# A fused attention and two-MLP kernel: statistics of the first MLP off VectorE's one-column operations, moe_w_out's scaling in one instruction, ScalarE's tables preloaded

## The chip, the core and the metric

The kernel runs on one core of a Trainium2 chip. The time is the device time of one execution in microseconds (us), the median of several runs. A profile is one execution recorded by the hardware profiler; its span runs from the first to the last instruction. TensorE is PE in the rows (PEld its weight loads), VectorE is DVE, ScalarE is ACT, GpSimd is POOL, and SP is the engine that issues the DMAs. L12 is line 12 of the kernel.

## The reference

Attention with a compressed memory (4 batches, 8 heads, 576 tokens, width 64) gives 2304 rows of 512 columns. Two MLPs follow. Only the first is touched:

```
h = x @ w_in                                   # 2304 x 1024
e = exp(h - max(h)); sm = e / (sum(e) + 1e-9)
solu = h * sm
mu = mean(solu); var = mean((solu - mu)**2)
ln = (solu - mu) / sqrt(var + 1e-6) * g_ln
x = ln @ w_out                                 # 2304 x 512
```

The second is `(sigmoid(x @ w_gate) * (x @ w_val)) @ w_out`. The weights arrive as 64-bit floats.

## The kernel before

Every matmul takes its operands as a high and a low part in fp32r and sums three products. The work has three stages: attention in 16 head pairs in a fixed order (up to 219 us), the first MLP (to 440 us), the second MLP in 6 passes over its width (to the end).

The first MLP (class `Moe1`) works in 18 tiles of 128 tokens. `hidden(t)` splits the input (`xs`, L594 on ScalarE, L595 on GpSimd for t below 6 and on VectorE after), multiplies it by w_in into a PSUM tile `h` (L602, 24 matmuls, two PSUM buffers), and takes the statistics: maximum (L609, VectorE), exp with its sum (L611, ScalarE), then sum plus 1e-9 and its reciprocal (L612, L613, VectorE, one column each), product with h and its sum (L615, VectorE; this read is the last one of the PSUM tile), minus the mean (L616, one column), squares and their sum (L619, ScalarE), variance plus 1e-6 (L620, VectorE, one column), the power -0.5 (L622, GpSimd, one column), mean times that (L623, VectorE, one column), and the normalised tile (L624, ScalarE). `lntrans(t)` transposes it on TensorE (L641, `pl`) and splits it into `lnT` (L138 on ScalarE, L139 on VectorE); `proj(g)` multiplies two tiles by w_out (L653, `po`).

Beside the first tiles runs the conversion of w_out (`w_out`, 8 blocks of 128x512, two staging buffers `raw` and `ex`): a DMA, two integer masks (L108, L109, VectorE), the exponent (L112, ScalarE), two products on VectorE (L119 mantissa, L117 exponent), then per block g_ln's scaling and the product of mantissa and exponent: for odd blocks both on GpSimd (L574, L575), for even ones the scaling on ScalarE (L577) and the product on GpSimd (L578). Then the high part (L580, ScalarE) and the low part `wol` (L145, GpSimd). The weights of the second MLP are converted in the same way later (L703 on VectorE, L142 and L145 on GpSimd).

The attention stage is written in its final order. After it a scheduler sets each engine's order from its own estimates; every engine then works through its queue in that order. `gl` holds g_ln: it is loaded by a DMA (L799) and scaled on VectorE (L800), and both come to stand in the attention stage.

Of the kernel before, what the change touches and what calls it, by code (L numbers as in the profile page):

```python
# [8 lines left out]
F32 = mybir.dt.float32  # L9
# [4 lines left out]
AF = mybir.ActivationFunctionType  # L14
ALU = mybir.AluOpType
AX = mybir.AxisListType
# [19 lines left out]
def f32(ap):  # L36
    return ap.bitcast(F32)
# [13 lines left out]
def kernel(  # L51
# [16 lines left out]
    nc = tc.nc  # L68
    B, H, S, D = q.shape
    NT, DM = out.shape  # L70
    F1 = moe_w_in.shape[1]
    F2 = moe2_w_gate.shape[1]
    P = 128
# [12 lines left out]
    cpool = ctx.enter_context(tc.tile_pool(name="cpool", bufs=1))  # L86
# [2 lines left out]
    make_identity(nc, ident)  # L89
    mhalf = cpool.tile([P, 1], F32, tag="mhalf", name="mhalf")  # L90
    nc.vector.memset(mhalf, -0.5)

    ebias = cpool.tile([P, 1], F32, tag="ebias", name="ebias")
    nc.vector.memset(ebias, -896.0 * 2.0**23)
# [29 lines left out]
    def load_f64(raw, ex, mt, src):  # L124
        load_raw(raw, src)
        f64_a(raw, ex, mt)
        f64_r(ex)
        f64_b(raw, ex, mt)
# [15 lines left out]
    def pool_lo(lo, src, hi):  # L144
        nc.gpsimd.tensor_sub(lo, src, f32(hi))  # L145
# [400 lines left out]
    class Moe1:  # L546
# [15 lines left out]
        def w_out(self, wp, stage, gl):  # L562

            self.wo = []
            for c in range(NF1):
                self.wo.append(
                    [wp.tile([P, DM], F32R, tag=f"wo{x}{c}", name=f"wo{x}{c}") for x in "hl"]
                )

            def one(c):  # L570
                raw, ex, m = staged(stage, f"wo{c}")
                load_f64(raw, ex[:, 0], ex[:, 1], moe_w_out[c * P : c * P + P, :].unsqueeze(1))
                if c % 2:
                    nc.gpsimd.tensor_scalar(m, m, gl[:, c : c + 1], 1.0, ALU.mult, ALU.mult)  # L574
                    nc.gpsimd.tensor_mul(m, m, f32(ex[:, 0]))  # L575
                else:
                    nc.scalar.activation(m, m, AF.Copy, scale=gl[:, c : c + 1])  # L577
                    nc.gpsimd.tensor_mul(m, m, f32(ex[:, 0]))  # L578
                hi, lo = self.wo[c]
                nc.scalar.copy(hi, m)  # L580
                pool_lo(lo, m, hi)

            return [lambda c=c: one(c) for c in range(NF1)]

        def hidden(self, t):
            sb = self.sb
            xs = self.xe.tile([P, 2, NC, P], F32R, tag="xs", name=f"xs{t}")
            e = self.xe.tile([P, F1], F32, tag="e", name=f"e{t}")
            ph = self.ps.tile([P, F1], F32, tag="h", name=f"h{t}", bufs=2)

            def xsplit():
                hi, lo = (xs[:, i].rearrange("p c (n t) -> p n c t", t=64) for i in range(2))
                src = X[:, 2 * t : 2 * t + 2]
                nc.scalar.copy(hi, src)  # L594
                (nc.gpsimd if t < 6 else nc.vector).tensor_sub(lo, src, f32(hi))  # L595

            def mm(c):
                hi, lo = self.wi[c]
                for s, ws in ((0, (hi, lo)), (1, (hi,))):
                    for w in ws:  # L600
                        for j in range(2):
                            nc.tensor.matmul(  # L602
                                ph[:, j * 512 : j * 512 + 512], xs[:, s, c], w[:, j * 512 : j * 512 + 512],
                                start=(c == 0 and s == 0 and w is hi), stop=(c == NC - 1 and s == 1),
                            )

            def stats():
                nm = sb.tile([P, 1], F32, tag="hm", name=f"hm{t}", bufs=2)
                self.last = nc.vector.tensor_reduce(nm, ph, axis=AX.X, op=ALU.max, negate=True).ins  # L609
                sm = sb.tile([P, 1], F32, tag="sm", name=f"sm{t}", bufs=2)  # L610
                nc.scalar.activation(e, ph, AF.Exp, bias=nm, accum_out=sm)  # L611
                nc.vector.tensor_scalar_add(sm, sm, 1e-9)  # L612
                nc.vector.reciprocal(sm, sm)  # L613
                mu = sb.tile([P, 1], F32, tag="mu", name=f"mu{t}", bufs=2)
                nc.vector.scalar_tensor_tensor(e, ph, sm, e, ALU.mult, ALU.mult, accum_out=mu)  # L615
                nc.vector.tensor_scalar_mul(mu, mu, -1.0 / F1)  # L616
                va = sb.tile([P, 1], F32, tag="va", name=f"va{t}", bufs=2)
                sq = sb.tile([P, F1], BF16, tag="sq", name=f"sq{t}", bufs=1)
                nc.scalar.activation(sq, e, AF.Square, bias=mu, accum_out=va)  # L619
                nc.vector.tensor_scalar(va, va, 1.0 / F1, 1e-6, ALU.mult, ALU.add)  # L620
                rd = sb.tile([P, 1], F32, tag="rd", name=f"rd{t}", bufs=2)
                nc.gpsimd.tensor_tensor(rd, va, mhalf, ALU.pow)  # L622
                nc.vector.tensor_mul(mu, mu, rd)  # L623
                nc.scalar.activation(e, e, AF.Identity, bias=mu, scale=rd)  # L624
                self.ln[t] = e

            return [xsplit, *(lambda c=c: mm(c) for c in range(NC)), stats]
# [157 lines left out]
    def staged(pool, nm):  # L785
        raw = pool.tile([P, 512, 2], I32, tag="raw", name=f"raw{nm}")
        ex = pool.tile([P, 2, 512], I32, tag="ex", name=f"ex{nm}")
        return raw, ex, f32(ex[:, 1])
# [4 lines left out]
    gl = cpool.tile([P, NF1], F32, tag="gl", name="gl")  # L793
# [63 lines left out]
```

## Time and profile before

| | us |
|---|---|
| median of 3 runs | 900.95 |
| lowest and highest | 899.72, 902.34 |
| the profiled execution, its time | 900.28 |
| its span | 898.4 |
| TensorE busy | 869.9 (97%) |
| VectorE busy | 555.1 (62%) |
| ScalarE busy | 419.4 (47%) |
| GpSimd busy | 273.1 (30%) |

Busy shares are means over three stages with different limits. A matmul's end is modelled, so a busy TensorE is not one at its peak. What a stage is worth is read from that stage's own waits.

### The profile page before, as it was taken

The page shows a single profiled execution, that of the slowest core. Times are in us where ns is not written, and L with a number is a line of the kernel's source. Part 1 is how long each engine was busy: PE and PEld are TensorE (multiplying, and loading weights), DVE is VectorE, ACT ScalarE, POOL GpSimd, SP SyncE. Part 2 cuts the span into 40 slices and gives each one's busy share as a digit, 9 for nine tenths or more (in the row PEclk, how much of TensorE's full clock was granted, in tenths as well). Part 3 has the DMA queues.
Part 4 walks back from the last instruction along what each step waited for, and adds up shares of the span by engine and source line. Part 5 has one row for each costly group of instructions (what it writes and reads, how often), then busy time and mean ns, then how long its engine had stood idle before and what let it go on. Part 6 is the DMA issues. An engine that isn't in the chain of part 4 may idle for free.

```text
span 898.4 us, 13966 instructions
## 1 busy us (share of the span) xinstructions
PE 869.9 (97%) x5224; PEld 724.4 (81%) x5224; DVE 555.1 (62%) x1317; ACT 419.4 (47%) x925; POOL 273.1 (30%) x320
## 2 busy tenths in 40 slices
PE   5999999999789999999999999999999999999998
PEld 3777777766678999999898888888888888888887
DVE  5899999995775554948642168365359635343334
ACT  4899999995765555654453242112113111111110
POOL 3777777784744111204200042040025012000000
PEclk9999999999979999999999999999999999999999
DMA  5543444420212000301200022011003100000113
GB/s 118 114 107 91 112 98 107 116 85 25 71 48 71 24 25 24 92 4 49 93 2 0 1 94 94 1 48 47 1 24 117 48 0 1 1 1 1 47 47 117
DMA packets 76291, 48.62 MB, mean 54 GB/s; under 512 B 62656, under 2 KB 62656, under 8 KB 76224
## 3 DMA queue, kind: packets, MB, share of 16 engines
q1 hardware_dynamic: 76224, 47.74, 19.1%
q8 instruction: 41, 0.67, 0.3%
q14 instruction: 26, 0.21, 0.1%
HBM read 43.00 MB, written 4.72 MB: 53 GB/s over the span
## 4 chain that ended last, share of the span: by engine, by line
PE 88%; DVE 6%; POOL 2%; issue 1%; DMA 1%; ACT 1%; SPq 0%; POOLq 0%; DVEq 0%; ACTq 0%
PE gv L735 33%; PE po L754 16%; PE po L653 9%; PE h L602 7%; PE x L464 5%; PE sc L355 4%; PE x L449 2%; PE sc L346 1%; PE pl L641 1%; PE trk L265 1%; PE trq L265 1%; PE trf L265 1%; DVE hm L609 1%; DVE exwo L119 1%; DVE exwo L108 1%
## 5 line engine op out<-in xcount | busy, mean ns | idle before, releaser
L741 DVE TENSOR_TENSOR sg<-sg,gv 128x512 f32<-128x512 f32 (+1 forms) x60 | 37.9, 632 | 176.6 <-ACT sg L740 176.6
L740 ACT ACTIVATE sg<-gv 128x512 f32<-128x512 f32 (+1 forms) x60 | 33.1, 552 | 234.5 <-PE gv L735 234.5
L735 PE MATMUL gv<-xx,gh 128*128 128x512 f32 (+1 forms) x480 | 136.1, 368 | 0.2 <-ACT xx L138 0.2
L735 PE MATMUL gv<-xx,vh 128*128 128x512 f32 (+1 forms) x480 | 136.0, 368 | 0.0
L653 PE MATMUL po<-lnT,woh 128*128 128x256 f32 x576 | 107.2, 288 | 3.8 <-DVE lnT L139 3.0
L735 PEld LDWEIGHTS gv<-xx,gh 128*128 128x128 f32 x480 | 87.4, 188 | 16.1 <-issue 0.4
L735 PEld LDWEIGHTS gv<-xx,vh 128*128 128x128 f32 x480 | 87.1, 189 | 15.0
L653 PEld LDWEIGHTS po<-lnT,woh 128*128 128x128 f32 x576 | 92.2, 195 | 5.6 <-DVE lnT L139 3.4
L394 POOL TENSOR_SCALAR p<-p,rs,o 128x256 f32<-128x256 f32 (+2 forms) x144 | 91.8, 652 | 11.6 <-ACT q L280 6.1
L735 PE MATMUL gv<-xx,gl 128*128 128x512 f32 (+1 forms) x240 | 88.3, 368 | 0.0
L735 PE MATMUL gv<-xx,vl 128*128 128x512 f32 (+1 forms) x240 | 88.3, 368 | 0.0
L384 ACT ACTIVATE p<-p,nm 128x128 f32<-128x128 f32 (+2 forms) x144 | 82.8, 584 | 5.1 <-DVE nm L377 5.1
L754 PE MATMUL po<-oh,GVxs 128*128 128x512 f32 x216 | 84.1, 389 | 0.0
L754 PE MATMUL po<-ol,GVxs 128*128 128x512 f32 x216 | 84.1, 389 | 0.0
L754 PE MATMUL po<-oh,GVe 128*128 128x512 f32 x216 | 84.0, 389 | 0.0
L602 PE MATMUL h<-wih,xs 128*128 128x512 f32 x288 | 81.2, 395 | 2.8 <-DVE e L615 2.8
L653 PE MATMUL po<-lnT,wol 128*128 128x256 f32 x288 | 82.1, 287 | 0.0
L761 DVE TENSOR_TENSOR X<-X,po 128x512 f32<-128x512 f32 x90 | 61.3, 683 | 23.2 <-PE po L754 23.2
L602 PEld LDWEIGHTS h<-wih,xs 128*128 128x128 f32 x288 | 52.8, 188 | 14.0 <-ACT e L624 2.9
L142 POOL TENSOR_SCALAR gh<-exg 128x512 fp32r<-128x512 f32 x12 | 8.8, 746 | 181.0 <-PE gv L735 142.1
L138 ACT CAST GVxs<-sg 128x512 fp32r<-128x512 f32 (+1 forms) x60 | 34.8, 579 | 46.5 <-DVE sg L741 46.5
L653 PEld LDWEIGHTS po<-lnT,wol 128*128 128x128 f32 x288 | 56.0, 195 | 0.2
(352 smaller groups left out, 1762.0 us busy)
## 6 DMA issues: line engine op xcount, KB each, us to landing
rawg<-in_moe_w_gate_dram SPq DMA_DIRECT2D x12, 512.0 KB, 3.8
rawv<-in_moe_w_val_dram SPq DMA_DIRECT2D x12, 512.0 KB, 3.8
rawo<-in_moe_w_out_dram SPq DMA_DIRECT2D x12, 512.0 KB, 3.5
out_dram<-X SPq DMA_DIRECT2D x18, 256.0 KB, 2.0
qt<-in_q_dram SPq DMA_DIRECT2D x32, 128.0 KB, 2.7
kt<-in_k_dram SPq DMA_DIRECT2D x32, 128.0 KB, 2.6
vt<-in_v_dram SPq DMA_DIRECT2D x32, 128.0 KB, 2.6
raw<-in_moe_w_in_dram SPq DMA_DIRECT2D x16, 256.0 KB, 3.4
```

The source lines that it names most:

```text
L138: nc.scalar.copy(hi, src)
L355: nc.tensor.matmul(ps[:, hh, :w], q2[sl, c, w - P : w], kk[sl, :w], start=m == 0, stop=m == 2)
L384: nc.scalar.activation(p, p, AF.Exp, bias=nm, scale=-1.0, accum_out=self.sum[n % 2][:, c, 0:1])
L394: nc.gpsimd.tensor_scalar(p, p, r["rs"][:, c : c + 1], og, ALU.mult, ALU.mult)
L464: nc.tensor.matmul(r["x", g][64 * hh : 64 * hh + 64, c0 : c0 + src.shape[1]], r["vt"][:, c : c + D], src, start=False, stop=j == 0,)
L602: nc.tensor.matmul(ph[:, j * 512 : j * 512 + 512], xs[:, s, c], w[:, j * 512 : j * 512 + 512], start=(c == 0 and s == 0 and w is hi), stop ...
L653: nc.tensor.matmul(po[:, :GW], w[:, m * P : m * P + P], L[:, x, c], start=(c == 0 and n == 0), stop=(c == NF1 - 1 and n == 2),)
L735: nc.tensor.matmul(ps[:, j, :w], wt[:, c, fs], xx[:, x, c], start=(c == 0 and n == 0), stop=(c == NC - 1 and n == 2),)
L740: nc.scalar.activation(sg[:, :w], ps[:, 0, :w], AF.Sigmoid)
L741: nc.vector.tensor_mul(sg[:, :w], sg[:, :w], ps[:, 1, :w])
L754: nc.tensor.matmul(po, GV[x][:, f, sl], wt[:, f], start=(f == 0 and n == 0), stop=(f == NCH - 1 and n == 2),)
L761: nc.vector.tensor_add(acc[:, t], acc[:, t], po)
```

## The change

Three edits. First, an Exp of one column into a tile of its own stands at the head of the kernel, so that ScalarE's tables are loaded there. Second, in the conversion of w_out the scaling by g_ln and the product become one VectorE instruction for all blocks. Third, the statistics: the sum of exps and a filled 1e-9 lie in two columns of one tile (filled by GpSimd) and are added by a reduction; the mean's negation and division go into the scale of the square and of a later factor, and the variance and the mean's factor are computed on GpSimd beside the power. `mu` is replaced by `su`, the plain sum.

```
--- before.py
+++ after.py
@@ -90,6 +90,9 @@
     mhalf = cpool.tile([P, 1], F32, tag="mhalf", name="mhalf")
     nc.vector.memset(mhalf, -0.5)
 
+
+    nc.scalar.activation(cpool.tile([P, 1], F32, tag="warm", name="warm"), mhalf, AF.Exp)
+
     ebias = cpool.tile([P, 1], F32, tag="ebias", name="ebias")
     nc.vector.memset(ebias, -896.0 * 2.0**23)
     moe_w_in, moe_w_out, moe2_w_gate, moe2_w_val, moe2_w_out = (
@@ -570,12 +573,7 @@
             def one(c):
                 raw, ex, m = staged(stage, f"wo{c}")
                 load_f64(raw, ex[:, 0], ex[:, 1], moe_w_out[c * P : c * P + P, :].unsqueeze(1))
-                if c % 2:
-                    nc.gpsimd.tensor_scalar(m, m, gl[:, c : c + 1], 1.0, ALU.mult, ALU.mult)
-                    nc.gpsimd.tensor_mul(m, m, f32(ex[:, 0]))
-                else:
-                    nc.scalar.activation(m, m, AF.Copy, scale=gl[:, c : c + 1])
-                    nc.gpsimd.tensor_mul(m, m, f32(ex[:, 0]))
+                nc.vector.scalar_tensor_tensor(m, m, gl[:, c : c + 1], f32(ex[:, 0]), ALU.mult, ALU.mult)
                 hi, lo = self.wo[c]
                 nc.scalar.copy(hi, m)
                 pool_lo(lo, m, hi)
@@ -607,21 +605,24 @@
             def stats():
                 nm = sb.tile([P, 1], F32, tag="hm", name=f"hm{t}", bufs=2)
                 self.last = nc.vector.tensor_reduce(nm, ph, axis=AX.X, op=ALU.max, negate=True).ins
-                sm = sb.tile([P, 1], F32, tag="sm", name=f"sm{t}", bufs=2)
-                nc.scalar.activation(e, ph, AF.Exp, bias=nm, accum_out=sm)
-                nc.vector.tensor_scalar_add(sm, sm, 1e-9)
-                nc.vector.reciprocal(sm, sm)
-                mu = sb.tile([P, 1], F32, tag="mu", name=f"mu{t}", bufs=2)
-                nc.vector.scalar_tensor_tensor(e, ph, sm, e, ALU.mult, ALU.mult, accum_out=mu)
-                nc.vector.tensor_scalar_mul(mu, mu, -1.0 / F1)
+
+                sm = sb.tile([P, 2], F32, tag="sm", name=f"sm{t}", bufs=2)
+                nc.gpsimd.memset(sm[:, 1:], 1e-9)
+                nc.scalar.activation(e, ph, AF.Exp, bias=nm, accum_out=sm[:, 0:1])
+                rs = sb.tile([P, 1], F32, tag="rs", name=f"rs{t}", bufs=2)
+                nc.vector.reduce_sum(rs, sm, axis=AX.X)
+                nc.vector.reciprocal(rs, rs)
+
+                su = sb.tile([P, 1], F32, tag="su", name=f"su{t}", bufs=2)
+                nc.vector.scalar_tensor_tensor(e, ph, rs, e, ALU.mult, ALU.mult, accum_out=su)
                 va = sb.tile([P, 1], F32, tag="va", name=f"va{t}", bufs=2)
                 sq = sb.tile([P, F1], BF16, tag="sq", name=f"sq{t}", bufs=1)
-                nc.scalar.activation(sq, e, AF.Square, bias=mu, accum_out=va)
-                nc.vector.tensor_scalar(va, va, 1.0 / F1, 1e-6, ALU.mult, ALU.add)
+                nc.scalar.activation(sq, e, AF.Square, bias=su, scale=-1.0 * F1, accum_out=va)
+                nc.gpsimd.tensor_scalar(va, va, 1.0 / F1**3, 1e-6, ALU.mult, ALU.add)
                 rd = sb.tile([P, 1], F32, tag="rd", name=f"rd{t}", bufs=2)
                 nc.gpsimd.tensor_tensor(rd, va, mhalf, ALU.pow)
-                nc.vector.tensor_mul(mu, mu, rd)
-                nc.scalar.activation(e, e, AF.Identity, bias=mu, scale=rd)
+                nc.gpsimd.tensor_scalar(su, su, rd, -1.0 / F1, ALU.mult, ALU.mult)
+                nc.scalar.activation(e, e, AF.Identity, bias=su, scale=rd)
                 self.ln[t] = e
 
             return [xsplit, *(lambda c=c: mm(c) for c in range(NC)), stats]
```

The orders change from 219 us on; up to there they are the same but for the two ScalarE instructions at the head. Two places follow. In them `exwo2` is the staged block 2 of w_out, `hm0` the maximum of tile 0, `sm0` its sum, `rs0` the reciprocal's tile, `e0` its exps, `xs2` the split input of tile 2, `wol0` the low part of block 0.

VectorE, from the maximum of tile 0 to the maximum of tile 1, before:

```order
L609 TENSOR_REDUCE hm0_3664<-h0_3562 128x1
L612 TENSOR_SCALAR sm0_3666<-sm0_3666 128x1
L613 RECIPROCAL sm0_3666<-sm0_3666 128x1
L615 SCALAR_TENSOR_TENSOR e0_3561,mu0_3670<-h0_3562,sm0_3666,e0_3561 128x1024
L108 TENSOR_SCALAR exwo2_3682<-rawwo2_3681 128x512
L109 TENSOR_SCALAR exwo2_3682<-rawwo2_3681 128x512
L616 TENSOR_SCALAR mu0_3670<-mu0_3670 128x1
L609 TENSOR_REDUCE hm1_3719<-h1_3565 128x1
```

The same place now (the lines have moved by one to three: L609 is L607, L615 is L617, L108 is L111):

```order
L607 TENSOR_REDUCE hm0_3664<-h0_3564 128x1
L576 SCALAR_TENSOR_TENSOR exwo1_3628<-exwo1_3628,gl_84 128x512
L111 TENSOR_SCALAR exwo2_3683<-rawwo2_3682 128x512
L112 TENSOR_SCALAR exwo2_3683<-rawwo2_3682 128x512
L613 TENSOR_REDUCE rs0_3669<-sm0_3666 128x1
L122 SCALAR_TENSOR_TENSOR exwo2_3683<-rawwo2_3682,exwo2_3683 128x512
L614 RECIPROCAL rs0_3669<-rs0_3669 128x1
L120 SCALAR_TENSOR_TENSOR exwo2_3683<-rawwo2_3682,exwo2_3683 128x512
L617 SCALAR_TENSOR_TENSOR e0_3563,su0_3672<-h0_3564,rs0_3669,e0_3563 128x1024
L607 TENSOR_REDUCE hm1_3719<-h1_3567 128x1
```

The product of tile 0 stood right behind its reciprocal and ahead of block 2's masks; now it stands behind block 2's masks and products, and block 1's new product is ahead of them all.

GpSimd, from the first instruction of the first MLP, before:

```order
L578 TENSOR_TENSOR exwo0_3615<-exwo0_3615 128x512
L574 TENSOR_SCALAR exwo1_3627<-exwo1_3627,gl_82 128x512
L595 TENSOR_TENSOR xs2_3566<-X_67,xs2_3566 128x2x4x64
L575 TENSOR_TENSOR exwo1_3627<-exwo1_3627 128x512
L145 TENSOR_TENSOR wol0_3545<-exwo0_3615,woh0_3544 128x512
L145 TENSOR_TENSOR wol1_3547<-exwo1_3627,woh1_3546 128x512
L595 TENSOR_TENSOR xs3_3569<-X_67,xs3_3569 128x2x4x64
L622 TENSOR_TENSOR rd0_3677<-va0_3673,mhalf_63 128x1
```

The same place now:

```order
L610 MEMSET sm0_3666 128x1
L610 MEMSET sm1_3721 128x1
L593 TENSOR_TENSOR xs2_3568<-X_69,xs2_3568 128x2x4x64
L148 TENSOR_TENSOR wol0_3547<-exwo0_3617,woh0_3546 128x512
L610 MEMSET sm2_3791 128x1
L148 TENSOR_TENSOR wol1_3549<-exwo1_3628,woh1_3548 128x512
L593 TENSOR_TENSOR xs3_3571<-X_69,xs3_3571 128x2x4x64
L621 TENSOR_SCALAR va0_3674<-va0_3674 128x1
L623 TENSOR_TENSOR rd0_3678<-va0_3674,mhalf_63 128x1
L624 TENSOR_SCALAR su0_3672<-su0_3672,rd0_3678 128x1
```

The scalings and products of w_out are gone from GpSimd's queue, the fills of `sm` stand in it (that of tile 2 ahead of the low part of block 1), and the power has a scaling on either side.

## Rows read from the trace of the kernel before

**Rows 1.** Stretches: start:end, length, busy us (and instructions) of PE, PEld, DVE, ACT, POOL, clock, DMA, GB/s

```profile
219.20:276.00 56.80, 48.19 (x230) 40.14 (x229) 46.71 (x85) 37.81 (x60) 32.93 (x28) 0.91 0.22 74
290.00:325.00 35.00, 35.00 (x241) 32.40 (x241) 22.37 (x50) 22.26 (x39) 5.44 (x7) 1.00 0.10 31
480.00:898.00 418.00, 414.48 (x1964) 348.77 (x1962) 200.17 (x314) 86.33 (x149) 53.48 (x48) 1.00 0.11 37
```

**Rows 2.** Waits of PE, 219 to 276 us: waiter, releaser, us, times, longest

```profile
PE po L653 <- DVE lnT L139: 3.0, 1, 3.0
PE h L602 <- DVE e L615: 2.8, 2, 2.5
PE pl L641 <- ACT e L624: 2.2, 1, 2.2
PE po L653 <- ACT woh L580: 0.6, 1, 0.6
```

**Rows 3.** Stretches with their clock, columns as in rows 1

```profile
249.00:257.50 8.50, 5.51 (x26) 5.27 (x26) 7.64 (x18) 5.59 (x9) 5.57 (x7) 0.52 0.19 66
257.50:260.00 2.50, 2.50 (x13) 2.07 (x12) 1.12 (x3) 1.78 (x4) 1.43 (x2) 1.00 0.00 0
```

**Rows 4.** The chain that ended last: start us, us, engine, tile, line, count

```profile
252.19 5.20 PE po L653 x23
...
284.23 5.76 PE po L653 x48
```

**Rows 5.** Timeline of DVE: start us, us, line, operation, tiles, shapes, idle before

```profile
227.91 1.28 DVE L615 SCALAR_TENSOR_TENSOR e<-h,sm,e 128x1024 f32<-128x1024 f32 x1
...
229.50 1.50 DVE L108 TENSOR_SCALAR exwo<-rawwo 128x512 int32<-128x512 int32 x1 [0.30 <-POOL wol L145]
...
235.52 1.22 DVE L623 TENSOR_TENSOR mu<-mu,rd 128x1 f32<-128x1 f32 x1 [0.39 <-POOL rd L622]
```

**Rows 6.** Timeline of POOL over the same time

```profile
225.67 1.29 POOL L595 TENSOR_TENSOR xs<-X,xs 128x512 fp32r<-128x512 f32 x1 [0.33 <-ACT xs L594]
...
228.18 2.54 POOL L145 TENSOR_TENSOR wol<-exwo,woh 128x512 fp32r<-128x512 f32 x2
...
235.46 1.26 POOL L578 TENSOR_TENSOR exwo<-exwo 128x512 f32<-128x512 f32 x1
```

**Rows 7.** Groups, 215 to 470 us: count | busy us, mean ns | idle before, releasers

```profile
L622 POOL TENSOR_TENSOR rd<-va,mhalf 128x1 f32<-128x1 f32 x18 | 12.3, 685 | 51.8 <-DVE va L620 51.1 <-DVE sm L612 0.7
...
L623 DVE TENSOR_TENSOR mu<-mu,rd 128x1 f32<-128x1 f32 x18 | 7.6, 420 | 9.0 <-POOL rd L622 9.0
...
L575 POOL TENSOR_TENSOR exwo<-exwo 128x512 f32<-128x512 f32 x4 | 5.6, 1400 | 1.8 <-DVE exwo L117 1.8
...
L616 DVE TENSOR_SCALAR mu<-mu 128x1 f32<-128x1 f32 x18 | 2.6, 147 | 0.1
...
L142 POOL TENSOR_SCALAR vh<-exv 128x512 fp32r<-128x512 f32 x4 | 2.5, 616 | 18.8 <-DVE mu L616 16.1 <-DVE exv L703 2.7
```

**Rows 8.** Line 703, whole span: shortest, median, longest in ns, first and last start

```profile
L703 DVE SCALAR_TENSOR_TENSOR exg<-exg x12: 680/682/1511, 283.8 to 693.5; 128x512 f32<-128x512 f32 x12
```

**Rows 9.** Timeline of ACT at the start

```profile
5.14 1.28 ACT L300 ACT_TABLE_LOAD   x1 [5.14 <-DMA qt<-in_q_dram]
...
6.43 0.74 ACT L300 ACTIVATE E<-qt 128x640 f32<-128x640 f32 x1
```

**Rows 10.** Timeline of DVE, the scaling of gl

```profile
19.64 0.17 DVE L800 TENSOR_SCALAR gl<-gl 128x8 f32<-128x8 f32 x1 [2.58 <-DMA gl<-in_moe_g_ln_dram]
```

**Rows 11.** Timeline of SP's queue, the load of gl

```profile
16.51 0.43 SPq L799 DMA_DIRECT2D gl<-in_moe_g_ln_dram  x1
```

**Rows 12.** Line 388, whole span, columns as in rows 8

```profile
L388 DVE TENSOR_REDUCE rs<-sum x48: 143/154/157, 16.9 to 209.1; 128x4 f32<-128x8 f32 x32, 128x1 f32<-128x2 f32 x16
```

**Rows 13.** Groups of POOL, whole span, columns as in rows 7

```profile
L394 POOL TENSOR_SCALAR p<-p,rs,o 128x128 f32<-128x128 f32 x32 | 14.0, 448 | 0.0
...
L841 POOL MEMSET const-float32-0.0<- 128x1 f32 x1 | 0.1, 99 | 0.2 <-issue 0.2
```

## The prediction

> **What bounds the kernel now.** I read the busy time by stretches first, then what TensorE waited for, then single instructions on VectorE and GpSimd. From 290 us on TensorE is busy in every microsecond of a stretch in the first MLP, and in the second MLP in 414.48 of 418 us [rows 1]: there nothing that this change touches sets the time. The stretch from 219.2 to 276 us, the first tiles of the first MLP, is different: TensorE is busy 48.19 of 56.80 us, VectorE 46.71. What ends TensorE's waits there is listed in [rows 2]: 3.0 us for the transposed LayerNorm result, 2.8 for the exp-times-hidden product that frees a PSUM tile, 2.2 for the normalised tile, 0.6 for a moe_w_out block, together 8.6 us. All four come out of the statistics or the weight conversion. On top, the granted clock was 0.52 from 249 to 257.5 us and 1.00 right after [rows 3], that is, the 1.2 GHz level after TensorE had stood for 2.2 and 3.0 us close to each other. 23 projection matmuls took 5.20 us there, 0.226 each, where 48 took 5.76 us (0.120 each) at the full clock [rows 4]: 23 x 0.106 = 2.4 us lost. So about 11 us of 900 can be won here, and no more.
>
> VectorE stands at the centre of it because it and GpSimd shut each other out. The integer mask L108 at 229.50 us took 1.50 us, ending when GpSimd's two subtractions (228.18, 2.54 us) ended; the one-column product L623 at 235.52 took 1.22 us, as long as GpSimd's multiply that began at 235.46 with 1.26 us [rows 5, 6]. Undisturbed, a one-column VectorE operation takes 0.15 us [rows 7].
>
> **The change, part by part.**
>
> *Table preload.* The load of 1.28 us sits at 5.14 us, between the arrival of q and the first Exp at 6.43 [rows 9]; after the change it is done long before q lands. But VectorE then stands 2.58 us, until 19.64, for the DMA of gl, whose scaling (L800) is in its queue there [rows 10], and that DMA is issued by SyncE at 16.51 us, behind loads that do not wait for ScalarE's exps for more than about a tenth [rows 11]. VectorE would come 1.28 us earlier and wait 1.28 us longer. Bounds -1.28 and 0; I take -0.1, next to the wait row. The order of all engines up to 219 us is otherwise the old one.
>
> *moe_w_out.* Per block GpSimd loses its multiply, 1.40 us by L575 [rows 7], every second block also a scaling (0.62 us by the 512-column GpSimd scaling L142), and ScalarE the other scalings: GpSimd sheds 8 x 1.40 + 4 x 0.62 = 13.7 us. VectorE gains 8 products of two SBUF tensors; the nearest is L703, same shape, median 0.68 us [rows 8]: +5.4 us on the engine that is short.
>
> *Statistics.* Per tile VectorE loses three one-column operations (L616, L620, L623), 0.45 us, and with L623 its waits for GpSimd: that group's mean is 0.42 us, 0.26 over the undisturbed one [rows 7]. The 1e-9 addition becomes a reduction of two columns; the same form as L388 took 143 to 157 ns in all 48 cases [rows 12], so it costs what it replaces and never waited for GpSimd. Over the 7 tiles of the stage VectorE sheds 3.2 us and about as much again in waits; against +5.4 it comes out about even. GpSimd gains three operations per tile. A one-column fill took 0.10 us, the power 0.69 us with its waits, and a two-factor scaling of 128 columns 0.45 us [rows 7, 13]; between 128 and 512 columns (0.62 us) that is 0.44 ns per column, which leaves 0.39 us for one column. I take 0.39 for each of the two scalings, bounds 0.10 and 0.55. In 7 tiles GpSimd gains 7 x 0.88 = 6.2 us and still ends 7.5 us lighter.
>
> *New waits.* Two follow from the order shown above. The fill of sm2 must wait until rs0 has been read out of the same buffer, and the subtraction of block 1 stands behind it on GpSimd. And VectorE now has the masks and products of block 2 between hm0 and the product of tile 0, whose masks wait until GpSimd is through with block 0. I followed both orders through all engines with the durations of the rows (an instruction starts when its engine is free and what it reads or overwrites is done; VectorE's operations on SBUF alone and GpSimd's wait for each other). The first step in the new one: xs2 on GpSimd 225.6 to 226.8 (225.67 in [rows 6]), then the scaled product of block 1 on VectorE, wol0 to 228.7, masks to 229.4, L122 to 230.1, then wol1 on GpSimd has the port until 231.4, L120 to 232.0, product of tile 0 to 233.3. In the old trace that product was done at 229.19 [rows 5]. TensorE, through with tile 1 at 230.1, waits 3.3 us for tile 0's PSUM where it did not wait before. After that the new order is better: 1.1 us at 239.7 (product of tile 1), 2.2 at 246.2 (tile 2), 1.9 at 254.8 (transposed tile 1), 1.3 at 268.8 (block 6): 9.8 us. The same walk of the old order gives 12.5 us where the trace has 8.6 idle and 2.4 of slow clock, so it is some 1.5 us too high, on both sides as I take it. Term: 9.8 - 12.5 = -2.7 us. With both scalings at 0.10 us the new sum is 8.2 (-4.3), at 0.55 it is 10.8 (-1.7).
>
> First what the trace shows: L703, which also multiplies two SBUF tensors, took 0.68 us at the median and 1.51 at most, and L108 was held to 1.50 us [rows 5, 8]. The walk lets the new product wait like that. If it did not wait, the sum would be 6.2 us of idle, -6.3 instead of -2.7.
> The Trainium skill, SBUF — State Buffer, section SBUF: two separate sides, speaks against this edit: a VectorE operation with two SBUF inputs and a GpSimd operation hold one port pair exclusively, whoever comes first, for the whole instruction. The rows above agree with it. By that rule the term is the -2.7.
>
> *Clock.* The old stage lost 2.4 us to the slow level after stalls of 2.2 and 3.0 us that stood 2 us apart. The new stalls stand 5 us or more apart, but the first is longer than any of the old. Bounds: -2.4 (no fall) and 0 (as before); I take half, -1.2.
>
> *Cover.* In the later tiles the new GpSimd operations, 1.4 us per tile in a chain with the power, lie beside TensorE's full stretch, where GpSimd is busy 5.44 of 35 us [rows 1]: nothing. Without that cover they would cost 0.4 us per tile.
>
> **Sum.** -0.1 - 2.7 - 1.2 = -4.0 us. The profiled execution took 900.28 us, 1.9 more than its span; the median of the three runs is 900.95, 0.67 above it. I forecast 900.95 - 4.0 = 897.0 us.
>
> **Rivals.** *The stalls only move.* Three one-column operations per tile on GpSimd at 0.55 us each give -1.7; with a clock that falls as before nothing else, and 0.1 for the preload: 899.2 us. For it: the first stall of 3.3 us is new, and VectorE's load does not fall. Against it: GpSimd is 7.5 us lighter, so the holds in [rows 5] become fewer. 0.27.
>
> *VectorE gets the longer queue: slower.* If the holds do not become fewer, because a small GpSimd operation stands in the way as often as a long one did, VectorE has +5.4 - 3.2 = +2.2 us more work in the stage that it bounds, and a hold of some 0.3 us for each of the 8 products, +2.4: 905.5 us. It decides when more than about half of the eight products meet a running GpSimd operation. For it: GpSimd is busy 32.93 of 56.80 us [rows 1]. Against it: the power and its neighbours are short. 0.13.
>
> *The preload reaches the end.* If the gl wait ends earlier too, the 1.28 us come on top: 897.0 - 1.2 = 895.8. The first Exp starts right at the end of the load, 5.14 + 1.28 [rows 9], so nothing more than that can be saved. 0.05.
> The Trainium skill, ScalarE: Activation LUTs, section What ACT_TABLE_LOAD costs, gives a switch 2.66 us with a drain; by it this rival would give 894.4. The rows show 1.28 and no gap behind it.
>
> **How the numbers follow.** Forecast 0.55, stalls move 0.27, slower 0.13, preload 0.05. About 0.3%, 2.7 us, is what a measurement of this kernel can tell from no change. Faster by more than that: 0.55 + 0.05 = 0.60; within: 0.27; slower: 0.13. The range reaches at the lower end to -6.3 with the clock term and the preload, 900.95 - 7.6, rounded to 893.0, at the upper end past the second case to no change, 901.0.
>
> **What would show it.** Right: the first projection of the stage starts later than before but with idle before it under 2.5 us; TensorE's idle from 219 to 276 us falls from 8.6 to 6 to 9 us with fewer slow stretches; a new wait of the third hidden tile for the product L617 near 230 us, 2 to 3.5 us; L800 waits about 3.7 us instead of 2.58 and the first projection tiles gain nothing from the preload; one-column VectorE operations with more than 0.2 us vanish. Wrong: the two scalings on GpSimd well over 0.55 us, the new product with a mean over 1 us, or idle in TensorE after 290 us.

## The result and the profile after

The changed kernel takes 894.06 us (median of 5 runs, 892.26 to 894.36) beside 900.97 us for the kernel before on the same chip: a ratio of 0.9916 with a 95% interval of 0.9903 to 0.993, or 6.3 to 8.7 us less. The forecast was 897.0 with a range of 893.0 to 901.0. The profiled execution took 892.26 us with a span of 890.4, 8.0 us less than the span before.

The whole difference lies in the first MLP. Stretches of both kernels, columns as in [rows 1]; of before, from the first matmul of the first MLP to the first one of the second, the slow stretch, and the rest:

```profile
219.19:439.79 220.60, 211.53 (x1346) 191.24 (x1345) 146.90 (x294) 123.99 (x208) 66.75 (x66) 0.98 0.16 53
246.90:257.20 10.30, 7.12 (x31) 6.44 (x32) 9.44 (x20) 7.13 (x13) 6.49 (x7) 0.50 0.30 103
439.79:898.40 458.61, 454.69 (x2184) 383.77 (x2184) 216.89 (x342) 105.15 (x186) 53.48 (x48) 1.00 0.10 34
```

The same of after, and its stretch that answers to the first line of [rows 1]:

```profile
219.12:431.90 212.78, 208.64 (x1346) 189.48 (x1345) 144.16 (x248) 120.35 (x204) 68.20 (x106) 0.99 0.17 54
233.00:236.40 3.40, 3.27 (x8) 2.64 (x9) 3.40 (x8) 3.38 (x7) 1.81 (x4) 0.55 0.36 142
431.90:890.40 458.50, 454.69 (x2184) 383.76 (x2184) 216.10 (x342) 105.15 (x186) 54.12 (x48) 1.00 0.11 34
219.20:276.00 56.80, 52.86 (x267) 44.50 (x268) 51.69 (x86) 39.12 (x63) 27.79 (x36) 0.97 0.23 75
```

The attention ends as before (219.19 and 219.12), the second MLP is as long as before (458.61 and 458.50), and between them 220.60 us became 212.78: 7.8 us. TensorE's idle went from 220.60 - 211.53 = 9.07 to 4.14 us, 4.9 less. Its 1346 matmuls took 2.9 us less. The clock was at 0.55 for 3.4 us where it had been at 0.50 for 10.3, and some 2.0 of the 2.9 us can be assigned to that (worked out in the part on the prediction). VectorE is busier in the stretch up to 276 us than before (51.69 for 46.71): its busy share told nothing of what it cost.

What TensorE waited for from 219 to 276 us, the answer to [rows 2], and the two places in its timeline (start, us, what, idle before):

```profile
PE h L600 <- DVE e L617: 3.9, 2, 2.8
...
233.13 1.19 PE L600 MATMUL h<-wih,xs 128*128 128x512 f32 x2 [2.84 <-DVE e L617]
...
247.66 0.70 PE L600 MATMUL h<-wih,xs 128*128 128x512 f32 x2 [1.10 <-DVE e L617]
```

Four kinds of waits became one. The waits for the normalised tile (2.2 us), for its transposed copy (3.0) and for a weight block (0.6) are gone, and the first stall is the new one that the prediction placed at 230 us.

### The profile page after: what moved, and what is told of

It is laid out like the page before. It is cut to its first block, busy times and chain, and to the rows that moved or that the text cites. A ratio compares the mean times of both kernels' runs of the same rounds, so it can differ in the third digit from the quotient of the medians.

```text
span 890.4 us, 13982 instructions
## 1 busy us (share of the span) xinstructions
PE 867.3 (97%) x5224; PEld 723.1 (81%) x5224; DVE 553.0 (62%) x1271; ACT 416.2 (47%) x922; POOL 275.4 (31%) x362
## 4 chain that ended last, share of the span: by engine, by line
PE 94%; DVE 2%; POOL 1%; issue 1%; DMA 1%; SPq 0%; ACT 0%; POOLq 0%
PE gv L736 33%; PE po L755 17%; PE po L654 12%; PE h L600 10%; PE x L467 5%; PE sc L358 4%; PE x L452 2%; PE pl L642 2%; PE sc L349 1%; PE trk L268 1%; PE trq L268 1%; PE trf L268 1%; POOL p L397 1%; POOL xs L593 0%; PE t15b L419 0%
## 5 line engine op out<-in xcount | busy, mean ns | idle before, releaser
L654 PE MATMUL po<-lnT,woh 128*128 128x256 f32 x576 | 104.7, 284 | 0.0
L654 PEld LDWEIGHTS po<-lnT,woh 128*128 128x128 f32 x576 | 90.2, 192 | 0.9
L380 DVE CUSTOM_DVE_ANT_0 p<-sc,mask 128x128 f32<-128x128 f32 (+3 forms) x128 | 54.6, 479 | 1.7 <-PE sc L358 1.7
```

What stands on the lines that cost most here:

```text
L380: nc.vector.tensor_tensor_reduce(p, x, m, -1.0, 3.0e38, ALU.add, ALU.min, nm)
L654: nc.tensor.matmul(po[:, :GW], w[:, m * P : m * P + P], L[:, x, c], start=(c == 0 and n == 0), stop=(c == NF1 - 1 and n == 2),)
```

## The experiments

The letters in the expectations stand for: A, GpSimd's long operations hold VectorE; B, the load on VectorE's queue counts; C, the gain is an accident of the order that each text gets; Q, a tile's small operations wait for their turn in VectorE's queue. Ratios are to the kernel before in the same call, with 95% intervals.

### Each edit alone, and all but the preload

The kernel before with the first hunk of the change alone:

> The kernel before with the table preload alone. If the wait of gl's scaling takes back what the earlier first Exp gives, as the prediction has it: within 0.3 us of before, the load of 1.28 us near 0.7 us, and the scaling of gl still at about 19.7 us. If the preload reached the end (the rival): 1.2 us faster.

Measured (e1): 901.12 us, 1.0003 (0.9994 to 1.0012).

The kernel before with the second hunk alone:

> The kernel before with moe_w_out's single VectorE instruction alone. Theory A (GpSimd's long operations hold VectorE, and taking 13.7 us of them away is what counts): 4 us faster or more of the 6.9 measured for all three edits. Theory B (VectorE's queue counts, and this edit puts 5.4 us on it): no faster than before, up to 2 us slower. Theory C (the gain is an accident of the order that each text happens to get): neither, and the single edits don't add up to the whole.

Measured (e2): 900.58 us, 0.9996 (0.9985 to 1.0007).

The kernel before with the third hunk alone:

> The kernel before with the new statistics alone; the old products of moe_w_out stay on GpSimd, which now also gets the fills and the two scalings. Theory A: under 2 us faster, perhaps slower, since GpSimd becomes 6 us busier in the stage. Theory B (VectorE's one-column operations count): 4 us faster or more. Theory C: the sum of this run and the one with the products alone misses -6.9 us by over 2 us.

Measured (e3): 893.78 us, 0.9929 (0.9915 to 0.9943).

The change without the first hunk:

> The changed kernel without the preload: the products and the statistics together. If the preload is worth nothing: within 0.4 us of the changed kernel's 894.06, with TensorE's idle in the first MLP near the 4.1 us of the changed kernel. If the preload reached the end: 895.2 or more.

Measured (e4): 894.24 us, 0.9927 (0.9914 to 0.994), TensorE's idle in the first MLP 4.15 us.

The statistics alone bring what all three edits bring. The preload brings nothing that can be measured. The products bring nothing either, alone or on top of the statistics. GpSimd is the fifth engine in these lines, columns as in [rows 1], for the products alone and the statistics alone:

```profile
219.20:276.00 56.80, 49.14 (x237) 40.53 (x234) 47.53 (x89) 33.32 (x55) 19.36 (x16) 0.91 0.23 74
219.20:276.00 56.80, 52.48 (x267) 43.40 (x264) 44.53 (x71) 39.54 (x64) 39.55 (x45) 0.97 0.23 75
```

With GpSimd 13.6 us lighter than before (19.36 for 32.93) nothing is gained, and with GpSimd 6.6 us busier (39.55) everything. So A falls, and with it the picture that GpSimd's load was the main loss. C falls for these three by the test set for it: -6.4, -0.4 and +0.3 us add up to -6.5. With two of the three terms at nothing that is a weak test, and the order comes back below. But B does not follow yet: the products put 7.8 us on VectorE in the changed kernel (8 at a mean of 0.980) without harm. What TensorE waited for in the kernel with the products alone, 219 to 300 us:

```profile
PE pl L636 <- DVE lnT L139: 4.6, 1, 4.6
PE h L597 <- DVE e L610: 3.1, 2, 2.9
```

GpSimd's products are gone, and TensorE still waits 7.7 us for the statistics and what follows on them.

### The statistics in two parts

What the three removed operations did shows in the trace of before, beyond their 0.15 us. Timelines of VectorE and ScalarE for tile 0, from the end of its product ([rows 5]) to its square:

```profile
229.12 0.08 DVE L615 DVE_READ_ACCUMULATOR e<-h,sm,e 128x1 f32 x1
...
230.92 0.41 DVE L109 TENSOR_SCALAR exwo<-rawwo 128x512 int32<-128x512 int32 x1
231.26 0.14 DVE L616 TENSOR_SCALAR mu<-mu 128x1 f32<-128x1 f32 x1
...
230.41 0.62 ACT L594 CAST xs<-X 128x512 fp32r<-128x512 f32 x1 [1.55 <-PE h L602]
231.04 0.72 ACT L112 ACTIVATE exwo<-exwo,ebias 128x512 int32<-128x512 int32 x1
231.66 1.13 ACT L619 ACTIVATE sq<-e,mu 128x1024 bf16<-128x1024 f32 x1
```

The same of after:

```profile
231.70 1.27 DVE L617 SCALAR_TENSOR_TENSOR e<-h,rs,e 128x1024 f32<-128x1024 f32 x1
...
233.02 1.15 ACT L620 ACTIVATE sq<-e,su 128x1024 bf16<-128x1024 f32 x1 [2.07 <-DVE e L617]
```

Before, the product ends at 229.19, and the square starts 2.47 us later: it needs the negated mean (L616, 0.14 us), which stands in VectorE's queue behind the two masks of block 2, the first of which took 1.50 us where the second took 0.41. Not all of the 2.47 us is the mean's: two operations of ScalarE's own queue (L594, L112) stand ahead of the square until 231.76. In tiles 1 and 2 the square waits for the mean itself, and starts 1.85 and 1.30 us behind the product:

```profile
239.97 1.15 ACT L619 ACTIVATE sq<-e,mu 128x1024 bf16<-128x1024 f32 x1 [0.87 <-DVE mu L616]
...
254.63 1.15 ACT L619 ACTIVATE sq<-e,mu 128x1024 bf16<-128x1024 f32 x1 [2.46 <-DVE mu L616]
```

After, the square of tile 0 starts 0.05 us behind the product. Such an operation, small but needed by another engine, is called a link here. L620 and L623 are links too, on either side of the power. So the statistics edit was split at the links: L620 and L623 moved to GpSimd and nothing else,

```
-                nc.vector.tensor_scalar(va, va, 1.0 / F1, 1e-6, ALU.mult, ALU.add)
+                nc.gpsimd.tensor_scalar(va, va, 1.0 / F1, 1e-6, ALU.mult, ALU.add)
...
-                nc.vector.tensor_mul(mu, mu, rd)
+                nc.gpsimd.tensor_scalar(mu, mu, rd, 1.0, ALU.mult, ALU.mult)
```

> The kernel before with two of the one-column operations moved from VectorE to GpSimd, the variance's scaling and the mean times the factor, so that they stand beside the power; nothing else. Theory Q (what counts is that a tile's normalisation waits twice in VectorE's queue between the product and the power and again behind it, 7.6 us from product to normalised tile in the first two tiles): most of the 7.1 us of the whole statistics edit, 4 us faster or more, and 4 us or less from product to normalisation. Theory B (VectorE's load, operation by operation): two thirds of the three operations removed, 4.7 us; the two are told apart by the run without these two moves.

Measured (e5): 897.11 us, 0.9959 (0.9947 to 0.9971); product to square 2.47 and 2.23 us in the first two tiles, product to normalised tile 5.9 and 9.0 us, where theory Q asked for 4 or less.

Where a part of the gain comes from can be seen directly. VectorE up to the product of tile 1, and TensorE, which needs that product before it can write tile 3, before:

```profile
234.99 0.14 DVE L612 TENSOR_SCALAR sm<-sm 128x1 f32<-128x1 f32 x1
...
236.66 0.15 DVE L613 RECIPROCAL sm<-sm 128x1 f32<-128x1 f32 x1
236.84 1.28 DVE L615 SCALAR_TENSOR_TENSOR e<-h,sm,e 128x1024 f32<-128x1024 f32 x1
...
238.28 0.70 PE L602 MATMUL h<-wih,xs 128*128 128x512 f32 x2 [2.47 <-DVE e L615]
```

The same place in e5:

```profile
234.75 0.14 DVE L612 TENSOR_SCALAR sm<-sm 128x1 f32<-128x1 f32 x1
234.92 0.17 DVE L613 RECIPROCAL sm<-sm 128x1 f32<-128x1 f32 x1
235.12 1.28 DVE L615 SCALAR_TENSOR_TENSOR e<-h,sm,e 128x1024 f32<-128x1024 f32 x1
...
236.56 0.70 PE L602 MATMUL h<-wih,xs 128*128 128x512 f32 x2 [0.93 <-DVE e L615]
```

Before, the factor of tile 0 (L623, [rows 5]) stands between the two: VectorE is idle for 0.39 us until GpSimd's power is done, and the factor then takes 1.22 us. Without it tile 1's product comes 1.7 us earlier, and TensorE waits 0.93 us where it waited 2.47. So a link costs in two ways: it waits for what stands ahead of it, and what stands behind waits for it.

The statistics edit with these two left on VectorE:

```
-                nc.gpsimd.tensor_scalar(va, va, 1.0 / F1**3, 1e-6, ALU.mult, ALU.add)
+                nc.vector.tensor_scalar(va, va, 1.0 / F1**3, 1e-6, ALU.mult, ALU.add)
...
-                nc.gpsimd.tensor_scalar(su, su, rd, -1.0 / F1, ALU.mult, ALU.mult)
+                nc.vector.tensor_scalar(su, su, rd, -1.0 / F1, ALU.mult, ALU.mult)
```

> The kernel before with the rest of the statistics edit: the filled 1e-9 with the reduction, the mean folded into the square and the factor; the variance's scaling and the factor stay on VectorE. Theory Q: under 2 us faster, since the two links still stand in VectorE's queue. Theory B: one operation per tile less on VectorE, 2.4 us faster, a third of 7.1.

Measured (e6): 895.73 us, 0.9941 (0.9929 to 0.9953); product to square 0.04 and 0.89 us. Both theories had sized this part too small.

The same edit in the changed kernel, and the moves of the first diff together with the products:

> The changed kernel with the variance's scaling and the mean's factor put back on VectorE, all else as changed. Theory Q: nearly all of the gain is lost again, 898.5 us or more, and 7 us or more from product to normalisation in the first tiles. Theory B: a loss of 4.7 us at most with the products of moe_w_out at nothing: 898.8; or, if the products carry what the links don't, 895 to 896.

Measured (e7): 899.80 us, 0.9987 (0.9979 to 0.9995); product to normalised tile 4.1 and 8.9 us in the first two tiles.

> The kernel before with the variance's scaling and the mean's factor on GpSimd, and with moe_w_out's single VectorE instruction; the mean's negation stays on VectorE, between the product and the square. The products cost nothing with the whole statistics edit (893.78 without them, 894.24 with them) and 4 us where two links stayed on VectorE (895.73 and 899.80). Theory Q (a link that stays in VectorE's queue waits behind what the products add to it): one link is left, so the products take back 1 to 3 of the 3.7 us, 898 to 900. If the products cost nothing as soon as the links around the power are on GpSimd: 897.1, as without them.

Measured (e12): 901.54 us, 1.0004 (0.9995 to 1.0013); product to square 3.41 and 3.47 us.

Both my sizes for the parts were wrong. I had counted two links and forgotten the third, the negated mean. The edit that removes it (e6) brings 5.3 us, though not by that alone: it also brings the reduction, and turns the two-tensor factor L623 (up to 1.25 us on VectorE) into a scaling that took at most 0.216 us. The two moves around the power bring 3.7 us alone and some 1.1 on top of e6, which is within the intervals. And the products are not free: they cost nothing where no link is left on VectorE (e3 to e4), and 4.1 us where one or two are (0.9941 to 0.9987 from e6 to e7, where the preload comes with them, and 0.9959 to 1.0004 from e5 to e12).

Side by side, the ratios are these. The columns say which half of the statistics edit is in (the moves of L620 and L623, the rest, or both), the rows how w_out is scaled:

| | neither half | moves only | rest only | both |
|---|---|---|---|---|
| old products | 1 | 0.9959 (e5) | 0.9941 (e6) | 0.9929 (e3) |
| new products | 0.9996 (e2) | 1.0004 (e12) | 0.9987 (e7) | 0.9927 (e4) |

Beside the old products each half of the statistics edit pays by itself. Beside the new ones neither pays as much as 1 us by these ratios, and only both together do. Why that is so these runs do not show. Tile 0 and then tile 1 in the last kernel, VectorE and ScalarE:

```profile
234.92 0.09 DVE L610 DVE_READ_ACCUMULATOR e<-h,sm,e 128x1 f32 x1
234.92 1.22 DVE L604 TENSOR_REDUCE hm<-h 128x1 f32<-128x1024 f32 x1
236.06 0.42 DVE L108 TENSOR_SCALAR exwo<-rawwo 128x512 int32<-128x512 int32 x1
236.39 0.75 DVE L573 SCALAR_TENSOR_TENSOR exwo<-exwo,gl 128x512 f32<-128x512 f32 x1
237.05 0.42 DVE L109 TENSOR_SCALAR exwo<-rawwo 128x512 int32<-128x512 int32 x1
237.39 0.15 DVE L611 TENSOR_SCALAR mu<-mu 128x1 f32<-128x1 f32 x1
...
237.90 0.61 ACT L575 CAST woh<-exwo 128x512 fp32r<-128x512 f32 x1
238.41 1.15 ACT L614 ACTIVATE sq<-e,mu 128x1024 bf16<-128x1024 f32 x1
...
240.65 0.15 DVE L611 TENSOR_SCALAR mu<-mu 128x1 f32<-128x1 f32 x1
...
242.48 0.62 ACT L589 CAST xs<-X 128x512 fp32r<-128x512 f32 x1 [2.84 <-PE h L597]
```

In tile 0 the negated mean of 0.15 us stands behind 2.5 us of other work, one product among it. So a link pays for what stands ahead of it. In tile 1 it does not: the mean is done 0.7 us behind the product, and the square waits until 243.53 because a split of the input ahead of it in ScalarE's queue stood 2.84 us for TensorE. And theory Q does not rank all runs: with all three links on VectorE the products cost nothing (e2), and from product to normalised tile, tile 1 takes 7.7 us before, 8.2 in the kernel with the statistics alone, which is 6.4 us faster, and 8.9 with the links put back, which is 1.2 us faster; in e5, 3.7 us faster, it takes 9.0. Nor do the holds of L623 by GpSimd alone explain them: in e12 it is gone from VectorE, and nothing is gained. Each text also gets its own order on all engines, and how much of a difference is the order's, these runs can't tell apart: no two texts with different links had the same order.

### The fill, the early gl and the order

The changed kernel without the fill; the 1e-9 is added on VectorE:

```
-                nc.gpsimd.memset(sm[:, 1:], 1e-9)
...
-                nc.vector.reduce_sum(rs, sm, axis=AX.X)
+                nc.vector.tensor_scalar_add(rs, sm, 1e-9)
```

> The changed kernel without the fill: 1e-9 is added on VectorE again, one column to one column, in the place of the reduction; the orders of all engines are otherwise those of the changed kernel. If the fill's wait matters (GpSimd stood 0.98 us idle ahead of it at 229.6 us, with the low part of block 1 behind it, which then held VectorE for 1 us at 230.1): up to 1 us faster by the first stall of TensorE, 2.8 to 1.8, and up to 1.4 more by the clock. If it only moves the collision: within 0.4 us of the changed kernel.

Measured (e8): 893.46 us, 0.9916 (0.9902 to 0.993), within the intervals of the changed kernel; the first stall is 2.9 us. The fill's wait cost nothing that can be measured.

The changed kernel with the DMA of gl behind the first one of z, with and without the preload, and with blocks 2 to 7 of moe_w_out a tile later:

```
+            if n == 0:
+                nc.sync.dma_start(gl, moe_g_ln.rearrange("(c p) -> p c", p=P))
             r["z"] = self.zm[:, hp]
```

> The changed kernel with the load of gl issued behind the first load of z, near 5.4 us, in place of 16.5, and its scaling among VectorE's first operations; the orders of the first MLP are unchanged. In the changed kernel VectorE stood 2.91 us for gl, until 19.76, while the next score tile was ready at about 18.2. If that wait is on the path: 1.5 us faster than the changed kernel, 892.5. If TensorE's waits behind it end with something else: within 0.4 us of 894.06.

> The same without the preload: what the preload is worth once the wait for gl is gone. In the changed kernel the first Exp came 1.83 us earlier, but the first scores only 0.22 us earlier (12.81 for 13.03 us), since VectorE stood 0.52 us for ScalarE at 8.3 and its operation at 8.99 took 1.32 us. If that is all that is left: 0.2 us slower than the kernel with the preload and the early gl. If the preload's 1.28 us had been hidden by the wait for gl alone, as the prediction put it: 1.28 us slower.

> The kernel with the early gl, with blocks 2 to 7 of moe_w_out handed to the scheduler one tile later (with tiles 2, 3, 4, 4, 5, 5 in place of 1, 2, 3, 4, 5, 5), so that the product of tile 0 stands right behind its reciprocal again. If TensorE's first stall (2.84 us at 230 us, with 1.4 us of slow clock behind it) comes from the product's place in VectorE's queue: that stall is gone, and if nothing takes its place the kernel is 4 us faster than with the early gl alone. The rival: the conversion comes later and the wait moves to the transposes and to tile 4 (a walk with the rows' durations gives 0.4, 1.1, 0.8, 2.7 and 0.9 us there): 1.7 us faster by idle, and nothing where the clock falls after them.

Measured: 892.00 us, 0.9904 (0.9889 to 0.9918) with the early gl (e9); 893.08 us, 0.9908 (0.9893 to 0.9923) without the preload (e10); 892.04 us, 0.9902 (0.9888 to 0.9916) with the other order too (e11). None differs from the changed kernel, or from one another, by more than the intervals. The wait for gl is gone from 19.8 us, but its scaling now stands ahead in VectorE's queue at 9 us:

```profile
9.05 1.28 DVE L802 TENSOR_SCALAR gl<-gl 128x8 f32<-128x8 f32 x1 [1.25 <-DMA gl<-in_moe_g_ln_dram]
...
18.98 0.76 DVE L382 CUSTOM_DVE_ANT_1 p<-sc,mask 128x576 f32<-128x576 f32 x1 [1.03 <-PE sc L351]
```

It waits there for its DMA and then for GpSimd, and the score tile at 18.98 waits for TensorE. What of the 0.95 us that VectorE gains there (19.93 to 18.98) reaches the end these runs can't tell: by the ratios e9 is 1.1 us faster than the changed kernel, with intervals of 1.3 us on either side, so neither the 1.5 us expected nor nothing is excluded. With the other order the first stall is gone, and the wait moved, as the rival had it, and the slow clock moved with it (0.51 from 248.5 to 252.0 us). TensorE's waits in that kernel, 219 to 440 us:

```profile
PE h L602 <- DVE e L619: 2.3, 1, 2.3
PE pl L644 <- DVE rs L615: 0.5, 1, 0.5
PE pl L644 <- DVE lnT L142: 0.4, 1, 0.4
```

## Why the prediction was right, step by step

**The bound and its size: right.** "About 11 us of 900 can be won here, and no more": 7.8 were won, all in the named stage. That all of it "comes out of the statistics or the weight conversion" was half right: only out of the statistics.

**Idle, -2.7 forecast, -4.9 measured.** The walk gave the first stall closely (3.3 us at 230.1 forecast, 2.84 at 230.3 measured; the product done at 233.3 and 233.0) and had the one of tile 2 twice too long (2.2 at 246.2; 1.10 at 246.6). The stalls at 239.7, 254.8 and 268.8 did not come. So the walk's sum for the new order is the mis-sized term: 9.8 us where 4.1 was measured, against 12.5 for 9.1 in the old order. It was too high by 5.7 and by 3.4, and not by the same on both sides, as the prediction took it.

One place shows how. In the walk VectorE's operations on SBUF and GpSimd's wait for each other, and the product of tile 1 ends near 240.8 (the stall of 1.1 us at 239.7). It ended at 238.0. From 232.9 us on no VectorE operation ahead of it was held: the masks took 0.41 and 0.42 us, the new product 0.74, the two products of the conversion 0.69 and 0.68. GpSimd was the one that waited: beside them its power took 0.91 us and its second scaling 0.68, where the medians are 0.55 and 0.27. The price of the two scalings, taken as 0.39 us each, is not the reason: undisturbed they were cheaper, but the pair took 0.87, 0.88, 1.41 and 1.64 us in the first four tiles, more than 0.78. Why the stalls at 254.8 and 268.8 did not come stays open. Shortest, median and longest of the two scalings and of the new product, in ns:

```profile
L621 POOL TENSOR_SCALAR va<-va x18: 190/191/421, 234.3 to 416.1; 128x1 f32<-128x1 f32 x18
L624 POOL TENSOR_SCALAR su<-su,rd x18: 264/267/1351, 235.6 to 417.1; 128x1 f32<-128x1 f32 x18
L576 DVE SCALAR_TENSOR_TENSOR exwo<-exwo,gl x8: 739/746/1877, 222.3 to 263.7; 128x512 f32<-128x512 f32 x8
```

**What the walk hid.** It followed the order, so the links' turns in VectorE's queue were in its sum. The part on the statistics didn't say so: it priced the three operations at 0.45 us per tile and the hold of L623. It should have asked who waits for each of them and what stands ahead of it. Read in that way, it would have put most of the gain on the statistics and none on the products. The prediction's "VectorE and GpSimd shut each other out" is true in the rows (two of the eight new products took 1.40 and 1.88 us, a third 0.85; L108, read as ending with GpSimd's two subtractions, ended 0.28 us behind them), but a lighter GpSimd was not what paid. That was its argument against the first rival (7.5 us lighter; 5.1 measured, 27.79 for 32.93), and with the statistics alone GpSimd is 6.6 us busier than before and the gain is the same. That the forecast came out on the right side in spite of this argument is in part luck.

**Clock, -1.2 forecast, some -2 to -2.9 measured.** The bound was too narrow: of the old loss only the 23 projection matmuls were counted (2.4 us). The eight transposes at 247 us took 2.11 us in the slow stretch and 1.03 elsewhere, 1.1 more: 3.5 in all. The new loss is one fall after the 2.84 us stall: 8 matmuls in 3.27 us where two start every 0.46 us at the full clock, 8 in 1.8, so 1.5 us. That leaves -2.0; the other 0.9 of the 2.9 I could not assign. The sum also used the clock twice: the walk of the old order was set against 8.6 us of idle and 2.4 of slow clock together to find it 1.5 us too high, and the clock then had a term of its own.

**Preload, -0.1 forecast, nothing that can be told from noise measured (-0.5 to +1.1).** The size fits, the cover was right only in part. I forecast a wait of 3.7 us for gl; it was 2.91. VectorE had lost most of the lead before it came there, to ScalarE and to GpSimd. The new start, VectorE and GpSimd:

```profile
8.31 0.76 DVE L298 TENSOR_TENSOR kl<-trk,kh 128x576 fp32r<-128x576 f32 x1 [0.52 <-ACT kh L138]
8.99 1.32 DVE L209 TENSOR_SCALAR bt<-bt 128x8 f32<-128x8 f32 x1
...
19.76 0.17 DVE L801 TENSOR_SCALAR gl<-gl 128x8 f32<-128x8 f32 x1 [2.91 <-DMA gl<-in_moe_g_ln_dram]
...
8.73 1.55 POOL L313 TENSOR_TENSOR G<-E,zm 128x640 f32<-128x640 f32 x1 [5.34 <-DMA zm<-in_z_prev_dram]
```

L209 took 1.32 us, until GpSimd's product ended at 10.28 (before: 0.29 us). GpSimd starts when zm lands, and the preload does not move that. So gl was a second cover behind a first one. With gl out of the way part of the lead does live on: the score tile that starts at 18.98 us in e9 starts 0.82 us later without the preload (e10):

```profile
19.80 0.76 DVE L379 CUSTOM_DVE_ANT_1 p<-sc,mask 128x576 f32<-128x576 f32 x1 [1.61 <-PE sc L348]
```

Whether it reaches the end is not shown: the two kernels differ by 0.4 us in their ratios and 1.1 in their medians, with intervals of 1.3 us and more on either side. The end of the attention stage alone lies between 218.8 and 221.1 us in the traces of these runs.

**The rivals.** *The stalls only move* held for the first stall alone. *VectorE gets the longer queue* was given its turning point at half of the eight products; by their rows three met GpSimd. Its load was put at 5.4 us and came to 7.8. Its price was real in some kernels: the products cost 4 us beside either half of the statistics edit (e5 to e12, e6 to e7), and nothing beside the whole or none of it. *The preload reaches the end* did not happen. The new GpSimd chain is covered in the later tiles, as forecast: TensorE is busy in every microsecond from 290 to 325 us.

**The signs and the range.** Of the signs of being right, the new wait near 230 us came (2.84), and the first projection started later (254.08 for 252.19) with no idle before it. TensorE's idle from 219 to 276 us fell further than the 6 to 9 us named, to 3.9. A sign of being wrong came too: the scaling L624 took 0.68, 0.69, 1.22 and 1.35 us in the first four tiles, well over 0.55, and the kernel was faster than forecast all the same, so it did not tell what it was named for. The measured 894.06 lies close to the lower end of the range (893.35 by its own terms, given as 893.0). That end was worked out from new products that never wait for GpSimd, and three of eight did, so that the range reaches this far is in part luck too.

## What to carry to other kernels

Price a small operation by its turn, not by its length: ask what stands ahead of it in its engine's queue, and which engine waits for it. A link of 0.14 us on VectorE kept ScalarE's square 1.85 and 1.30 us behind the product in tiles 1 and 2 here, and one that stood idle for GpSimd kept the next tile's product back by 1.7. Folding one link into a scale that ScalarE applies anyway and moving the others beside the power paid 6.4 us together, while taking 13.6 us of work off GpSimd (32.9 to 19.4 in the stage, e2) paid nothing. And test the parts in the company that they will have: each half of the statistics edit paid alone, and neither did beside the new products.

## What the runs showed of the hardware

A two-factor GpSimd scaling of one column took 0.19 us with constants and 0.27 with one factor from memory when nothing held it, beside 0.45 for 128 columns [rows 13]; the longest took 1.35.

On VectorE, the one-column operations with constants (L612, L616, L620) took at most 0.157 us in all 54 cases of the kernel before, beside GpSimd or not, and the links put back there (e7, 36 cases) at most 0.217. The two-tensor L623 took up to 1.25 us, and an 8-column one with constants, L209, 1.32: it ended with GpSimd's operation. The Trainium skill, SBUF — State Buffer, section SBUF: two separate sides, names two kinds of VectorE operations that GpSimd shuts out, those with two SBUF inputs and those in a two-port mode; L623 agrees with the first, and L209, with one tensor as its input, could only be the second, which no run here shows by itself.

After a stall of 2.84 us TensorE's clock was at 0.55 for 3.4 us; after stalls of 2.19 and 2.99 us, their ends 5.1 us apart, it was at 0.50 for 10.3. The length of one stall does not tell what follows: behind a stall of 2.47 us in the kernel before it stayed at 1.00 (238.3 to 243.0 us), and behind one of 2.27 us in e11 it fell to 0.51 for 3.5 us.
